# Rotary attention with a squared-ReLU MLP: scale and bias carried inside g, two-step rotations, a new order

## The chip, the cores and the metric

The kernel runs on one core of a Trainium2 chip. TensorE (PE) does the matrix products, and its weight loads are counted apart (PEld). VectorE (DVE), ScalarE (ACT) and GpSimd (POOL) do the elementwise work. SyncE (SP) issues every DMA. The metric is the device time of one execution in microseconds.

## The reference, cut to what matters

```python
# q, k, v: (4, 8, 576, 64); x: 2304 tokens of 512; w_in: 512 x 2048; w_out: 2048 x 512; s, b: one number each
q_rot, k_rot = rotate(q), rotate(k)      # [x1*cos - x2*sin, x1*sin + x2*cos] on halves of 32
attn = softmax(q_rot @ k_rot.T / 8)      # rows of 576
x = (attn @ v) as 2304 x 512
h = x @ w_in
r = max(h, 0)
g = s * (r * r) + b
out = g @ w_out
```

## The kernel before

The 32 (batch, head) pairs are handled two heads at a time, as 16 pairs `pr`. For each pair q, k and v are loaded, q and k are rotated, transposed and multiplied into tiles of 128x576 scores (`s_tile`, `s_pair`). `s_max` (DVE) takes the negated maximum of each row, `s_exp` (ACT) the exponentials and their sums, `p_r` the reciprocals, and `p_a` and `p_b` write each probability as two fp16 halves. DMA transposes turn these round (`p_t`, `p_tt`), and `pv_sum` (PE) multiplies with v, which is split in two halves as well. Pairs 0 to 3 go partly through fp32 products instead.

The weights arrive as 32 loads of 512 KB in 64-bit words and are rebuilt as fp32 (`w_low`, `w_rebias`, `w_join`). `w_gram` and `w_tot` bound their size. After that, `w_hi` and `w_lo` split each fp32 weight in place into two scaled fp16 halves.

The MLP works in nine units `u` of 256 tokens. Unit 0 runs in fp32 while the weights are still fp32: `mlp_in0`, `mlp_r0` (ReLU, then square, on ACT) and `mlp_out0`, in 8 chunks of 128x512. Units 1 to 8 use the halves, and each product is three matmuls. In each of 8 chunks per unit, `mlp_in` writes a 128x512 PSUM bank, `mlp_r` (ACT) makes hr = r squared, `g_hi` (ACT or DVE) rounds it to fp16, `g_lo` (DVE or POOL) subtracts to get the remainder, and `mlp_out` multiplies both by w_out. `out_sum` multiplies the result by a scale and adds the bias row. `x_norm`, `x_add`, `x_sum` and `x_scale` choose the power of two for each unit.

The bias b times the sums of w_out's columns is one row of 512 numbers, made once. `bias_cols` sums the columns of all 32 halves of w_out with matmuls (L510), `bias_part` copies the result out, `bias_mm` adds up the partitions (L517) and `bias_out` puts the row, `bcs`, into SBUF. `add_bias` and `out_sum` use it.

A rotation takes three instructions on one engine: z = x * sin with halves swapped (L589), x = x * cos (L591), x = x + z (L593). The buffer z has two slots.

Every instruction's place is written out by hand in the string ORDER. PICKS says which engine does a piece that has a choice, and SLOTS says which buffer slot a tile takes. Each engine runs its instructions strictly in that order, and a semaphore makes it wait for another engine or a DMA. The scores have two PSUM tiles, the products of the first layer two banks, hr two buffers and g three. The lines L411, L413, L416 and L419 are helpers through which most DVE, POOL and ACT instructions go, so groups are told apart there by their tiles.

Of the kernel before, what the change touches and what calls it, by code (L numbers as in the profile page):

```python
# [21 lines left out]
P_SCALE = 2.0 ** 14  # L22
# [11 lines left out]
BUFS = {"s": 2, "bank": 2, "po": 1, "nat": 1, "ot": 1, "xc": 4, "xt": 1, "hr": 2, "k": 2, "q": 2, "v": 4, "z": 2, "p": 4, "pab": 6, "pt": 2, "x": 4,  # L34
# [40 lines left out]
    "Y2joYCX5j7YMYQkMYRYkYDj1kNYNX7Izj9Y3YgjqYOjyYcYSj0YlYnYdkVYmYokOkEYyYPj8X6kFYzYpj-YEY0YqkUYrkPYvj_YskWYwkHkXaMYtY4ZQYhZR"
    "aNZSY5Y6Y9aPY7kGYikhkIY-Y8kQkikSkjY_aQkkkJkYklkRaRjAkZkTYxkmaOknkokbkpkqkrZTksYuZgkaaSYjktkcn0kdaTaUkukeZUkvZVk4ZWkwZXZb"
    "kxZYk5kykzZjk6n1lWZkk7ZZlXn2k8k9lClYZhlZkflDaVn3k0lEn4k2lFk1lGk-ZllHlAn5Zin6Zck3n7k_n8n9n-lBn_lIZClMZDZFlNZGoAZHZAlOZmZn"
    "lPZoZrZuZalQl0ZvlRZsl1ZpZElJl2ZIZJlLZKZBl3lKZNl4lhZwlalglbZxoMliZyljZOlSZLZzlTZMlrZ0Z-ZdlVldZPlUlclkkgZ1lellZ2lfZ3Z5oLl5"
    "lnoNlqoOoPlmlsoQloZ_ltZeZ6lpZfZ4oglulvZtofZ7lxohoCoiZqoVlzoBl7oDlwoEaBaXlyl9oFl6oGl_oWaCaYl8Z8l-ojmAoIZ9aZaDopoXaWoYoKaA"
# [70 lines left out]
def plan():  # L150
# [32 lines left out]
    def prep(pr):  # L183
# [14 lines left out]
        for nm in "kq":  # L198
            add((DVE, POOL), "rotate", pr, nm, steps=3, r=[("tab",)], w=[(nm, pr), ("z", pr, nm)])
# [893 lines left out]
```

## Time and profile before

| what | value |
|---|---|
| median of 3 runs | 604.07 us (603.09 to 606.6) |
| profiled execution | 603.72 us, of which the span from first to last instruction is 601.9 us |
| PE busy | 575.6 us (96%) |
| DVE busy | 467.4 us (78%) |
| ACT busy | 400.6 us (67%) |
| POOL busy | 143.8 us (24%) |
| granted TensorE clock | 1.00, that is 2.4 GHz |

A busy share is an average over stages. The stretches in the rows below tell the stages apart: the loads and the first pairs, attention together with the MLP, and the MLP alone at the end. Mean durations include the time in which an instruction was held up by another engine. Neighbouring instructions of one engine overlap by a few hundredths of a microsecond, so a sum of durations is a little more than the busy time.

### The profile page before, as it was taken

The page shows a single profiled execution, that of the slowest core. Times are in us where ns is not written, and L with a number is a line of the kernel's source. Part 1 is how long each engine was busy: PE and PEld are TensorE (multiplying, and loading weights), DVE is VectorE, ACT ScalarE, POOL GpSimd, SP SyncE. Part 2 cuts the span into 40 slices and gives each one's busy share as a digit, 9 for nine tenths or more (in the row PEclk, how much of TensorE's full clock was granted, in tenths as well). Part 3 has the DMA queues.
Part 4 walks back from the last instruction along what each step waited for, and adds up shares of the span by engine and source line. Part 5 has one row for each costly group of instructions (what it writes and reads, how often), then busy time and mean ns, then how long its engine had stood idle before and what let it go on. Part 6 is the DMA issues. An engine that isn't in the chain of part 4 may idle for free.

```text
span 601.9 us, 12378 instructions
## 1 busy us (share of the span) xinstructions
PE 575.6 (96%) x4655; PEld 391.7 (65%) x4655; DVE 467.4 (78%) x975; ACT 400.6 (67%) x838; POOL 143.8 (24%) x138
## 2 busy tenths in 40 slices
PE   2799999899999999999999999999999999999997
PEld 1476767566576657666766586666756676666774
DVE  5898999999999999999989999796777752223101
ACT  3798878689899886786868686757656453324321
POOL 0153521334332312331402253100310022120000
PEclk9999999999999999999999999999999999999999
DMA  8999999975975589799778587657654016310100
GB/s 305 307 336 283 221 237 188 214 163 130 214 167 123 126 154 202 158 192 194 152 162 198 125 153 151 156 129 146 120 99 114 2 40 133 95 40 1 36 1 35
DMA packets 210011, 90.32 MB, mean 150 GB/s; under 512 B 192288, under 2 KB 196768, under 8 KB 209952
## 3 DMA queue, kind: packets, MB, share of 16 engines
q1 hardware_dynamic: 209952, 89.54, 64.3%
q8 instruction: 36, 0.59, 0.4%
q14 instruction: 23, 0.19, 0.1%
HBM read 31.97 MB, written 4.72 MB: 61 GB/s over the span
## 4 chain that ended last, share of the span: by engine, by line
PE 83%; DVE 7%; DMA 4%; ACT 3%; issue 2%; POOL 1%; SPq 0%; DVEq 0%; ACTq 0%
PE px L886 28%; PE po L962 25%; PE px L759 8%; PE s L672 8%; PE po L929 4%; PE px L912 4%; DMA x<-in_moe_w_in_dram 2%; DMA x<-in_moe_w_out_dram 2%; PE s L962 2%; DVE wio L416 2%; PE s L654 2%; ACT p L419 1%; PE s L673 1%; DVE pab L416 1%; ACT x L419 1%
## 5 line engine op out<-in xcount | busy, mean ns | idle before, releaser
L886 PE MATMUL px<-xa,wio 128*128 128x256 f16 x1536 | 180.2, 273 | 0.0
L962 PE MATMUL po<-wio,g 128*128 128x512 f16 x720 | 171.9, 379 | 0.5 <-DVE o L416 0.5
L886 PEld LDWEIGHTS <-wio 128*128 128x128 f16 x1536 | 148.0, 98 | 29.6 <-issue 1.6
L419 ACT ACTIVATE p<-s,nm 128x576 f32<-128x576 f32 x144 | 105.5, 734 | 60.1 <-DVE s L681 30.9
L416 DVE SCALAR_TENSOR_TENSOR pab<-p,sum,pab 128x576 f16<-128x576 f32 x136 | 118.7, 887 | 8.1 <-ACT pab L419 4.7
L962 PEld LDWEIGHTS <-g 128*128 128x128 f16 x816 | 75.6, 98 | 73.1 <-issue 3.8
L681 DVE TENSOR_SCALAR_CACHE_REDUCE s<-s,sc 128x576 f32<-128x576 f32 x108 | 87.2, 819 | 17.0 <-PE s L673 15.5
L904 POOL TENSOR_TENSOR g<-hr,g 128x512 f16<-128x512 f32 x36 | 44.5, 1239 | 175.2 <-DVE g L783 85.4
L419 ACT ACTIVATE hr<-px,xc 128x512 f32<-128x512 f32 x64 | 43.5, 681 | 59.3 <-PE px L886 42.1
L413 POOL TENSOR_SCALAR pab<-p,sum 128x576 f16<-128x576 f32 x44 | 38.9, 887 | 165.6 <-DVE sum L708 114.9
L419 ACT ACTIVATE pab<-p,sum 128x576 f16<-128x576 f32 x67 | 50.5, 767 | 18.2 <-DVE sum L708 16.4
L759 PE MATMUL px<-pt,v 128*64 128x320 f16 (+2 forms) x640 | 49.0, 281 | 0.6 <-DVE wmx L480 0.6
L904 DVE TENSOR_TENSOR g<-hr,g 128x512 f16<-128x512 f32 x28 | 19.2, 688 | 36.1 <-ACT g L419 35.8
L419 ACT ACTIVATE hr<-hr 128x512 f32<-128x512 f32 x68 | 42.7, 629 | 1.7
L672 PE MATMUL s<-qkT 128*128 128x512 f16 (+1 forms) x120 | 41.3, 382 | 1.8 <-ACT p L419 1.8
L672 PE MATMUL s<-kS,qkT 128*128 128x512 f16 (+1 forms) x120 | 41.3, 380 | 0.0
L759 PEld LDWEIGHTS <-v 128*64 128x64 f16 x640 | 32.8, 110 | 11.2 <-issue 8.4
L672 PEld LDWEIGHTS <-qkT 128*128 128x128 f16 (+1 forms) x240 | 22.6, 100 | 23.8 <-issue 4.8
L419 ACT ACTIVATE g<-hr 128x512 f16<-128x512 f32 x39 | 24.2, 625 | 13.6 <-PE po L962 10.9
L912 PE MATMUL px<-x,wio 128*128 128x128 f32 x256 | 31.8, 278 | 0.0
L912 PEld LDWEIGHTS px<-x,wio 128*128 128x128 f32 x256 | 30.0, 192 | 2.7 <-issue 1.9
L783 DVE CAST g<-hr 128x512 f16<-128x512 f32 x25 | 10.5, 419 | 23.9 <-PE po L962 15.0
(151 smaller groups left out, 826.3 us busy)
## 6 DMA issues: line engine op xcount, KB each, us to landing
x<-in_moe_w_in_dram SPq DMA_DIRECT2D x16, 512.0 KB, 5.5
x<-in_moe_w_out_dram SPq DMA_DIRECT2D x16, 512.0 KB, 4.7
st_v<-in_v_dram SPq DMA_DIRECT2D x16, 320.0 KB, 3.8
st_q<-in_q_dram SPq DMA_DIRECT2D x16, 288.0 KB, 4.1
st_k<-in_k_dram SPq DMA_DIRECT2D x16, 288.0 KB, 3.9
out_dram<-o SPq DMA_DIRECT2D x7, 512.0 KB, 3.3
kS<-qkT SPq DMA_DIRECT2D x24, 144.0 KB, 2.6
pt<-pab SPq DMA_TRANSPOSE x152, 3.0
```

Of the source, the lines that this page charges most:

```text
L413: eng.tensor_scalar(out=out, in0=in0, scalar1=s1, scalar2=s2, op0=op0, op1=op1)
L416: nc.vector.scalar_tensor_tensor(out=out, in0=in0, scalar=scalar, in1=in1, op0=op0, op1=op1)
L419: nc.scalar.activation(out=out, in_=in_, func=func, **kw)
L654: nc.tensor.matmul(ps[h][:, to], d["qF"][hh, t * P:(t + 1) * P], d["kF"][hh, keys], start=True, stop=True)
L672: nc.tensor.matmul(ps[rows, MAIN:2 * MAIN], lhs, kk[:, h:8:2], start=(n == 0), stop=(n == 1))
L681: nc.vector.tensor_scalar(out=T["s"], in0=T["s"], scalar1=st[pr]["es"], scalar2=None, op0=ALU.mult, op1=ALU.min, accum_out=T["nm"])
L759: nc.tensor.matmul(o[64 * h:64 * h + 64, c], v_rows(pr, h, k, z), p_rows(pr, 2 * (i // 4) + h)[:, k, c], start=((z, k) == todo[0]), stop=( ...
L886: nc.tensor.matmul(ph, w16[0][:, f, wz, cc], X["xa"][:, xz, c], start=(c == 0 and n == 0), stop=(c == NC - 1 and n == 2))
L904: (nc.vector if eng == DVE else nc.gpsimd).tensor_tensor(out=g[:, 1], in0=r, in1=g[:, 0], op=ALU.subtract)
L912: nc.tensor.matmul(ph, wi[:, f + 1, c * P:(c + 1) * P], xs[0]["x"][:, c, j * P:(j + 1) * P], start=(c == 0), stop=(c == NC - 1))
L929: nc.tensor.matmul(X["po"][:, j * DM:(j + 1) * DM], gs["h", j, f - f % 4][:, f % 4 * P:(f % 4 + 1) * P], wo[:, f + 1], start=(n == 1), sto ...
L962: nc.tensor.matmul(po, g[:, gz, jj], w16[1][:, f, wz, to], start=(n == 1 and i == 0), stop=(n == NF and i == 2))
```

## The change

The power of two and the sign in s are folded into the weights' inverse scale, and b, suitably scaled, is added to every element of g before the second product. That makes the sums over w_out's columns superfluous: `bias_cols`, `bias_part`, `bias_mm`, `bias_out` and `add_bias` go, and so does the dependence of `out_sum` on `bcs`. `g_hi` becomes an addition of a per-partition number with a rounding, and `g_lo` becomes (hr + b) - g_hi in one DVE instruction. Unit 0 gets an extra pass `mlp_b0` over each of its 8 chunks. `sb_scale`, 14 instructions on one or two columns in 9 steps, prepares the scales, and `x_scale` grows from 7 steps to 8. `out_sum` is now a plain scaling and may go to ACT.

A rotation now multiplies x, read twice, by a table of cosines and sines side by side into z (128x1152), and one addition of the two halves of z writes x. The table grows from 432 KB to 576 KB, and z becomes one slot of twice the size. The ORDER, PICKS and SLOTS strings are all new.

```diff
-BUFS = {... "z": 2, ...}
+BUFS = {... "z": 1, ...}
...
-            add((DVE, POOL), "rotate", pr, nm, steps=3, r=[("tab",)], w=[(nm, pr), ("z", pr, nm)])
+            add((DVE, POOL), "rotate", pr, nm, steps=2, r=[("tab",)], w=[(nm, pr), ("z", pr, nm)])
...
-    def bias():
-        add(PE, "bias_cols", r=[("w16", 1, f) for f in range(NF)], w=[("bank", "cols")])
-        add(ACT, "bias_part", r=[("bank", "cols")], w=[("bcs",)])
-        add(PE, "bias_mm", r=[("bcs",)], w=[("bank", "bias")])
-        add(ACT, "bias_out", r=[("bank", "bias"), ("wsc", 1)], w=[("bcs",)])
...
+                add((ACT, DVE), "mlp_b0", j, f, r=[("sc0",)], w=[hr])
...
-        add(DVE, "x_scale", u, steps=7, r=[("bank", "xn", u), ("wsc", 0), ("wsc", 1)], w=[("xc", u)])
+        add(DVE, "x_scale", u, steps=8, r=[("bank", "xn", u), ("wsc", 0), ("wsc", 1)], w=[("xc", u)])
...
-            add((ACT, DVE), "g_hi", u, f, r=[("hr", c)], p=[("g", c)])
-            add((DVE, POOL), "g_lo", u, f, r=[("hr", c)], w=[("g", c)])
+            add((ACT, DVE), "g_hi", u, f, r=[("hr", c), ("xc", u)], p=[("g", c)])
+            add(DVE, "g_lo", u, f, r=[("hr", c), ("xc", u)], w=[("g", c)])
...
-            add(DVE, "out_sum", u, j, r=[("pj", u, j), ("bcs",), ("xc", u)], ...)
+            add((ACT, DVE), "out_sum", u, j, r=[("pj", u, j), ("xc", u)], ...)
...
+    add(DVE, "sb_scale", steps=9, r=[("sb",)], w=[("sc0",)])
...
-    tab = const.tile([P, 9, 96], F32, name="tab")
+    tab = const.tile([P, 9, 2, D], F32, name="tab")
...
-        z = new(rp, "z", [P, 9, 2, 32], F32)
-        eng.tensor_tensor(out=z[:, :, ::-1], in0=x, in1=sin, op=ALU.mult)
-        yield
-        eng.tensor_tensor(out=x, in0=x, in1=cos, op=ALU.mult)
-        yield
-        eng.tensor_tensor(out=x, in0=x, in1=z, op=ALU.add)
+        z = new(rp, "z", [P, 9, 2, D], F32)[:, 0:n]
+        eng.tensor_tensor(out=z, in0=x[:, :, None].to_broadcast([P, n, 2, D]), in1=tab[:, g], op=ALU.mult)
+        yield
+        turned = z[:, :, 1].rearrange("p t (h e) -> p t h e", h=2)[:, :, ::-1]
+        eng.tensor_tensor(out=x.rearrange("p t (h e) -> p t h e", h=2), in0=z[:, :, 0].rearrange("p t (h e) -> p t h e", h=2), in1=turned, op=ALU.add)
...
+    def plus(eng, out, x, add):
+        if eng == ACT:
+            act(out, x, AF.Identity, bias=add)
+        else:
+            ts_(out, x, add, ALU.add)
...
-        (nc.vector if eng == DVE else nc.gpsimd).tensor_tensor(out=g[:, 1], in0=r, in1=g[:, 0], op=ALU.subtract)
+        nc.vector.scalar_tensor_tensor(
+            out=g[:, 1], in0=r, scalar=xs[u]["c"][:, 2:3], in1=g[:, 0], op0=ALU.add, op1=ALU.subtract)
...
-        stt(X["o", j], out_tile(u, j), X["c"][:, 1:2], bcs[:, to], ALU.mult, ALU.add)
+        cast(eng, X["o", j], out_tile(u, j), X["c"][:, 1:2])
```

What the new strings say can be counted, with the plan's numbering. The table gives instructions per engine, old to new, for the whole kernel and for two parts of the order: from its beginning to the first `mlp_in` of unit 1, and from there to the 108th `s_max`.

| piece, engine | whole kernel | to the first `mlp_in` | from there to the 108th `s_max` |
|---|---|---|---|
| `g_lo`, POOL | 36 to 0 | 0 | 21 to 0 |
| `g_lo`, DVE | 28 to 64 | 0 | 6 to 26 |
| `g_hi`, DVE | 25 to 21 | 0 | 12 to 3 |
| `rotate`, DVE | 81 to 50 | 39 to 26 | 36 to 19 |
| `rotate`, POOL | 15 to 14 | 9 to 7 | 6 to 7 |
| `out_sum`, `out_sum0`, `add_bias`, DVE | 19 to 8 | 0 | 8 to 3 |
| `out_sum`, ACT | 0 to 10 | 0 | 0 to 4 |
| `mlp_b0`, ACT | 0 to 8 | 0 to 8 | 0 |
| `w_low`, DVE | 5 to 10 | 5 to 10 | 0 |
| `p_a`, DVE | 25 to 23 | 4 to 0 | 11 to 9 |
| `p_a`, POOL | 44 to 52 | 11 to 13 | 17 to 25 |

The first DMAs of the old order are q of pair 0, the table with the identity matrix, and k of pair 0. In the new order the table and the identity come first, then q and k. On DVE the old order begins with the rotation steps q0, q1, k0, q2, k1, a `w_join`, k2; the new one with q0, q1, k0, k1, `w_join`. In the new order six of POOL's seven rotations are followed by one on DVE that needs the same z. The closest of these is pair 11: between the place of POOL's rotation of k and that of DVE's rotation of q, DVE has four `s_max`, one `p_r` and one `g_lo` to do.

## Rows read from the trace of the kernel before

**Rows 1.** Busy time of each engine by stretch: start:end, length, PE, PEld, DVE, ACT, POOL.

```profile
0.00:25.00 25.00, 9.94 (x49) 6.26 (x50) 17.73 (x30) 12.79 (x23) 2.66 (x6) 1.00 0.86 300
25.00:125.00 100.00, 95.46 (x859) 69.03 (x859) 95.99 (x191) 79.40 (x182) 35.47 (x34) 1.00 0.94 246
...
150.00:375.00 225.00, 222.99 (x1854) 148.23 (x1854) 214.88 (x462) 177.65 (x378) 65.56 (x59) 1.00 0.79 166
375.00:475.00 100.00, 100.00 (x788) 65.59 (x784) 77.76 (x169) 64.35 (x132) 13.84 (x15) 1.00 0.55 115
...
sum 602.00, PE 575.56 PEld 391.69 DVE 467.37 ACT 400.56 POOL 143.81; mean PE 82.22 PEld 55.96 DVE 66.77 ACT 57.22 POOL 20.54
```

**Rows 2.** Chain that ended last, first 130 us: start, length, what.

```profile
27.94 7.28 DMA x<-in_moe_w_in_dram
```

**Rows 3.** Instructions in order of time, first 15 us: start, length, engine, line.

```profile
4.77 0.76 DVE L589 TENSOR_TENSOR z<-st_q,tab 128x576 f32<-128x576 f32 x1 [3.60 <-DMA tab<-in_rope_dram]
...
7.88 0.76 DVE L589 TENSOR_TENSOR z<-st_k,tab 128x576 f32<-128x576 f32 x1 [1.56 <-DMA st_k<-in_k_dram]
...
11.01 0.75 DVE L593 TENSOR_TENSOR st_k<-st_k,z 128x576 f32<-128x576 f32 x1
...
11.82 1.12 PE L766 MATMUL s<-ident,st_k 128*128 128x128 f32 x4 [0.93 <-DVE st_k L593]
...
14.09 2.40 PE L654 MATMUL s<-qkT 64*128 64x512 f32 x8 [0.75 <-ACT qkT L419]
```

**Rows 4.** Instructions of PE in order of time, 213 to 220 us.

```profile
213.42 1.91 PE L510 MATMUL px<-wio,ones 128*32 128x512 f16 x32
215.66 0.38 PE L672 MATMUL s<-qkT 128*128 128x512 f16 x1 [0.33 <-ACT p L419]
...
217.19 0.27 PE L851 MATMUL px<-g,ones16b 128*128 128x256 bf16 x1 [0.24 <-ACT bcs L419]
...
218.44 1.02 PE L517 MATMUL px<-bcs,ones 128*128 128x512 f32 x2
219.30 2.10 PE L962 MATMUL po<-wio,g 128*128 128x512 f16 x9
```

**Rows 5.** Groups by line and form: count, busy us, mean ns, idle before.

```profile
L416 DVE SCALAR_TENSOR_TENSOR pab<-p,sum,pab 128x576 f16<-128x576 f32 x136 | 118.7, 887 | 8.1 <-ACT pab L419 4.7 <-POOL pab L413 2.9
...
L681 DVE TENSOR_SCALAR_CACHE_REDUCE s<-s,sc 128x576 f32<-128x576 f32 x108 | 87.2, 819 | 17.0 <-PE s L673 15.5 <-ACT hr L419 1.2
...
L904 POOL TENSOR_TENSOR g<-hr,g 128x512 f16<-128x512 f32 x36 | 44.5, 1239 | 175.2 <-DVE g L783 85.4 <-ACT g L419 72.0 <-DVE sum L708 7.2
...
L416 DVE SCALAR_TENSOR_TENSOR wio<-wio,wsc 128x512 f16<-128x512 f32 x32 | 26.8, 838 | 0.8 <-ACT wio L419 0.8
...
L419 ACT ACTIVATE g<-hr 128x512 f16<-128x512 f32 x39 | 24.2, 625 | 13.6 <-PE po L962 10.9 <-PE px L851 1.3 <-PE s L962 1.0
...
L904 DVE TENSOR_TENSOR g<-hr,g 128x512 f16<-128x512 f32 x28 | 19.2, 688 | 36.1 <-ACT g L419 35.8
...
L589 DVE TENSOR_TENSOR z<-st_k,tab 128x576 f32<-128x576 f32 x15 | 12.8, 850 | 1.6 <-DMA st_k<-in_k_dram 1.6
...
L416 DVE SCALAR_TENSOR_TENSOR o<-po,xc,bcs 128x512 f32<-128x512 f32 x15 | 11.1, 747 | 7.3 <-PE po L962 6.5 <-DMA out_dram<-o 0.8
...
L783 DVE CAST g<-hr 128x512 f16<-128x512 f32 x25 | 10.5, 419 | 23.9 <-PE po L962 15.0 <-ACT hr L419 8.9
...
L416 DVE SCALAR_TENSOR_TENSOR xa<-x,xs,xa 128x1024 f16<-128x1024 f32 x7 | 8.9, 1276 | 0.9 <-ACT xa L419 0.8
...
L589 POOL TENSOR_TENSOR z<-st_q,tab 128x576 f32<-128x576 f32 x4 | 6.6, 1645 | 3.0 <-DMA st_q<-in_q_dram 2.9
```

**Rows 6.** Instructions of DVE in order of time, 422 to 428 us.

```profile
421.83 0.81 DVE L416 SCALAR_TENSOR_TENSOR pab<-p,sum,pab 128x576 f16<-128x576 f32 x1
...
423.60 3.95 DVE L416 SCALAR_TENSOR_TENSOR pab<-p,sum,pab 128x576 f16<-128x576 f32 x3
```

**Rows 7.** Instructions of POOL in order of time, same stretch.

```profile
423.22 2.98 POOL L904 TENSOR_TENSOR g<-hr,g 128x512 f16<-128x512 f32 x2
```

More of the change, by code (lines that the diff above doesn't have):

```diff
@@ L280, in halve @@
             add(PE, "w_tot", which, r=[("top", which)], w=[("bank", "tot", which)])
-            add(DVE, "w_scale", which, steps=4, r=[("bank", "tot", which)] + ([("sb",)] if which else []), w=[("wsc", which)])
+            add(DVE, "w_scale", which, steps=4, r=[("bank", "tot", which), ("sc0",)], w=[("wsc", which)])
         old = [("w32", which, f - 1)] if f else [("w32", 0, NF - 1)] if which else []
@@ L284, in halve @@
         add(DVE, "w_lo", which, f, r=[("w32", which, f), ("wsc", which)], w=[("w16", which, f)])
-    def bias():
-        add(PE, "bias_cols", r=[("w16", 1, f) for f in range(NF)], w=[("bank", "cols")])
-        add(ACT, "bias_part", r=[("bank", "cols")], w=[("bcs",)])
-        add(PE, "bias_mm", r=[("bcs",)], w=[("bank", "bias")])
-        add(ACT, "bias_out", r=[("bank", "bias"), ("wsc", 1)], w=[("bcs",)])
-        for j in range(2):
-            add(DVE, "add_bias", j, r=[("bcs",), ("sb",)], w=[("o", 0, j)], p=[("ot", 0)])
-        add(DMA, "store", 0, (0, 1), r=[("o", 0, 0), ("o", 0, 1), ("ot", 0)])
     def unit0():
@@ L344, in plan @@
             halve(which, f)
-    bias()
     for u in range(1, NU):
@@ L448, in load_w, with sb_scale @@
         wst[which, f] = t
+    def sb_scale():
+        d, root, zero, sigma, b1, mag = (sc[:, i:i + 1] for i in range(6))
+        stt(mag, sb[:, 0:1], -1.0, sb[:, 0:1], ALU.mult, ALU.max)
+        yield
+        yield from pow2(d, mag, root)
+        ts_(zero, mag, 0.0, ALU.is_equal)
+        yield
+        ts_(root, root, 2.0 ** 13, ALU.mult)
+        stt(root, zero, 0.0, root, ALU.is_equal, ALU.mult)
+        ts_(d, d, 2.0 ** -13, ALU.mult)
+        yield
+        stt(sigma, sb[:, 0:1], d, d, ALU.mult, ALU.mult)
+        yield
+        nc.vector.tensor_tensor(out=sigma, in0=sigma, in1=zero, op=ALU.add)
+        yield
+        nc.vector.reciprocal(b1, sigma)
+        nc.vector.tensor_tensor(out=b1, in0=b1, in1=sb[:, 1:2], op=ALU.mult)
+        nc.vector.memset(xw[:, 0:1], 1.0 + 2.0 ** -6)
+        nc.vector.memset(xb[:, 0:1], 0.0)
+        stt(mag, b1, -1.0, b1, ALU.mult, ALU.max)
+        ts_(sc[:, 6:7], root, 1.0 / P_SCALE, ALU.mult)
+        ts_(xb[:, 1:2], mag, 4096.0 * (1.0 + 2.0 ** -6), ALU.mult, 2.0 ** -100, ALU.add)
     def w_low(which, f, eng):
@@ L504, in w_lo @@
         stt(d[:, 1], w32[which][:, f + 1], wsc[:, which:which + 1], d[:, 0], ALU.mult, ALU.subtract)
-    def bias_cols():
-        o = wst["b"] = bank()
-        for n in range(2 * NF):
-            g = slice(32 * (n % 4), 32 * (n % 4) + 32)
-            nc.tensor.matmul(o[g], ones16, w16[1][:, n // 2, n % 2], start=(n < 4), stop=(n >= 2 * NF - 4))
-    def bias_part():
-        act(bcs, wst["b"], AF.Copy, scale=1.0 / 32.0)
-    def bias_mm():
-        wst["b"] = bank()
-        nc.tensor.matmul(wst["b"], ones32, bcs, start=True, stop=True)
-    def bias_out():
-        act(bcs, wst["b"], AF.Copy, scale=sb[:, 3:4])
     st = {pr: {} for pr in range(NPAIR)}
```

177 lines of the change are left out of this document (88 added, 89 removed).

## The prediction

> **What bounds the kernel now.** I read the busy times by stretch first [rows 1]. The reader is to see three regimes. In the first 25 us PE works 9.9 us: it waits for the first loads and rotations. From 25 to 125 us PE is busy 95.5 of 100 us while DVE is busy 96.0 and the DMA engines 0.94, so three resources are full together. From 150 to 375 us PE is busy 223.0 of 225 and DVE 214.9; from 375 to 475 us PE is busy 100.0 of 100 while DVE falls to 78. The granted clock is 1.00 in every stretch, that is 2.4 GHz. PE is idle for about 26 us in all (601.9 less 575.6 [rows 1]), and more than half of that lies in the first 25 us. So time is gained by giving PE less to do, or by filling its holes in the first 125 us. Work added to DVE costs nothing after 375 us, and before that it has 10 us of room in 225.
>
> The chain that ended last says the same of the early part: it leads through loads of the weights, one of which takes 7.28 us from issue to landing [rows 2]. A load starts when a buffer comes free, so in this part DMA, ACT and DVE take turns in setting the pace.
>
> **The change part by part.** The sum is made against the profiled execution, 603.72 us, 0.35 under the median of the runs.
>
> *The bias row.* PE spends 1.91 us on `bias_cols` and 0.86 us from the start of `bias_mm` to that of the next matmul, and `x_sum` waits 0.24 us for the bank that ACT's `bcs` copy still reads [rows 4]. That is 3.0 us of PE at most. The matmul after `bias_cols` was held 0.33 us by ACT all the same [rows 4], so I take 2.7. The lower end is 1.1 (0.86 + 0.24), if the wait for ACT had lasted as long without `bias_cols`. From 375 us on PE has no idle time, so what it saves before that reaches the end: -2.7 us (-3.0 to -1.1).
>
> *The start.* The table is a third larger and now goes first, with q and k behind it, so the first rotation, which waited 3.60 us for the table, starts later: the 144 KB more are, at the 300 GB/s of this stretch [rows 1], 0.5 us. Against that, k's rotation took from 7.88 to 11.76 us because a step of q and a `w_join` stood between its steps [rows 3]. Now its two steps stand together and take about 1.38 + 0.75 us after a landing at about 8.4 us, so k's transposes start near 10.5 instead of 11.82 and the first score tile near 12.8 instead of 14.09 [rows 3]. The ends are -1.3 us and +0.5 us (the later table, and the loads behind it setting the pace [rows 2]); I take -0.5.
>
> *The early stretch, up to unit 1.* DVE loses a third of its rotation steps there (39 to 26). A set of three takes 3 x 0.75 = 2.25 us undisturbed [rows 3]. The new z step has 1152 elements; the nearest rows are 0.75 us for 576 and 1.28 us for 1024 elements [rows 3, 5]. The line through them gives 1.42; the ends are 1.28 and 2 x 0.75. I take 1.4, so a set takes 2.15 and 13 sets save 1.3 us. Five more `w_low` against four fewer `p_a` on DVE, all one-input instructions like the cast of 0.42 us [rows 5], give +0.4, and the 14 small instructions of `sb_scale` at most 0.42 each, more likely half of it: +3 us. That nearly cancels, +2 on 96. On ACT the eight `mlp_b0` cost 8 x 0.63 = 5.0 us [rows 5], beside 79.4 of 100 us used [rows 1]. Behind each `mlp_b0` on ACT's queue stand exponentials, and PE's `mlp_out0` waits for it; the cover is the score tiles and `w_gram` that PE has between. I take 0, with ends at +5.0 (no cover) and -4.5 (the whole PE idle time of this stretch [rows 1]).
>
> *The tight stretch, 160 to 375 us.* Here DVE counts. Up to the 108th `s_max` it has 20 more `g_lo`, and all are three-operand: 26 at 0.69 to 0.84 us, the latter being the row of the same form with its hold-ups; I take 0.76. Against six at 0.69 [rows 5] that is +15.6 us (+13.8 to +17.7). Rotations: 36 steps at 0.75 make 27.0 us; nine and a half sets of 2.15 make 20.4: -6.6. Eight bias additions at 0.75 become three one-input copies at 0.42 to 0.75 [rows 5]: -4.2. Nine fewer `g_hi` at 0.42 [rows 5]: -3.8. Two fewer `p_a`: -0.8. The sum is about 0, with ends at +3 and -2. So the subtractions come to DVE without a net load, and ACT takes the rest: nine `g_hi` at 0.63 and four `out_sum` at about the same are +8 us on 178 of 225 [rows 1, 5], where it has room.
>
> POOL loses 36 subtractions of 1.24 us [rows 5], 45 us. It gains eight `p_a`, about 6 us at DVE's 0.8 for such an instruction, and its seven rotations, with z up to twice the 1.65 us that 576 elements take [rows 5], make 7 x 4.95 = 35 us against 15 steps of 1.65 or 25 us. That matters to DVE: a `p_b` takes 0.81 us alone, but three in a row took 3.95 us while two POOL subtractions of 2.98 us together ran [rows 6, 7]. Over all 136 the mean is 0.89, that is 0.08 x 136 = 10 us of hold-up for 144 us of POOL work [rows 1, 5]. POOL will work some 29 us less (45 - 6 - 10), so about 2 us come back on DVE. The Trainium skill has a rule for this ("SBUF — State Buffer", section "Who interferes with whom"): a DVE instruction with two SBUF inputs contends with a GpSimd instruction that reads SBUF, and whichever issued second fully blocks. By the rows 2 us come back; by that rule every overlapping pair would cost a whole instruction, and the 36 subtractions gone could return up to 36 x 0.81 = 29 us. It also speaks against the change, since the new `g_lo` and the twice as long z step are themselves two-input. The row agrees that single instructions are blocked (3.95 us against 3 x 0.81).
>
> For PE I take -0.5 in this stretch; the most is its 2.0 us of idle time [rows 1], and the other end is +3.
>
> *The end* is left out: the last product, scaling and store follow one another as before, on PE at full speed.
>
> The sum: 603.72 - 2.7 - 0.5 + 0 - 0.5 = 600.0 us, or 600.4 beside the median of 604.07.
>
> **The rivals.** *The single z buffer ties POOL to DVE (slower).* A rotation on POOL now holds the only z for 1.65 + 3.3 us and its waits [rows 5], and the next rotation on DVE, a strict queue with the maxima behind it, must wait. At pair 11 DVE has four `s_max` at 0.82, a `g_lo` and a `p_r` to do meanwhile, about 4.2 us [rows 5]. If POOL takes longer than that, each microsecond over it stands on DVE where it is 96% full, and PE runs out of scores. Such a handover occurs six times; at two of them a full 5 us would be 10 us: 610 us. It decides from two stalls of about 3.5 us on. For it speaks that POOL's own instructions are held up too; against it, that most handovers seem to have far more work between them.
>
> *The saved PE time is eaten (same).* PE lacks 2.7 us of work, but the new order has its holes elsewhere, for instance behind the eight `mlp_b0`: half of their 5.0 us without cover leaves 600.4 + 2.5 = 602.9, all of it 605.4.
>
> *More than PE's own saving (faster).* If DVE gets back several microseconds from POOL and the first tile's 1.3 us carries through, the holes between 25 and 125 us (4.5 us) and in the tight stretch (2.0 us) close as well [rows 1]: 603.72 - 3.0 - 1.3 - 4.5 - 2.0 makes 593; half of the gain beyond the forecast, 597.
>
> **How the numbers follow.** About 0.5%, or 3 us, is what a measurement of this kernel can tell from no change; so faster is under 601.05 and slower over 607.1. The forecast (598 to 603) has 0.44, of which 0.28 is faster; saved time eaten (602 to 606) 0.20; the single z, or another new stall of that size (607 to 612), 0.20; the larger gain (593 to 598) 0.16. That gives 0.45 faster, 0.35 same, 0.20 slower. The range leaves out the lower part of the larger gain and the upper of the stalls: 594.5 to 608.5. The likeliest case's own range is 598 to 603.
>
> **What would show it.** Right: no PE work at lines of bias sums; the first score tile before 13.5 us; a z step on DVE near 1.4 us; DVE's `g_lo` at 0.7 to 0.8 us; DVE busy between 475 and 600 us clearly more than now, and PE full from 150 us on. Wrong: waits of DVE's z step on POOL of microseconds; PE idle before `mlp_out0` for ACT; PE idle of more than 5 us between 150 and 475 us. The prediction fails on the fast side if the holes in the first 125 us shrink by more than 2 us, since I give the new order no credit there.

## The result and the profile after

The changed kernel takes 607.66 us (median of 14 runs, 605.23 to 610.75) against 603.84 us (14 runs beside them). The ratio is 1.0074 [1.0051, 1.0098]: slower by about 4.5 us (the two medians lie 3.8 apart). The forecast was 600.4 us, faster. The profiled execution has a span of 608.0 us and 609.82 us in all, 2.2 over the median.

The busy times by stretch, which answer to [rows 1], come first (columns as there; behind POOL stand the granted clock, the DMA share and GB/s):

```profile
0.00:25.00 25.00, 11.99 (x65) 7.77 (x66) 18.32 (x28) 12.15 (x22) 1.60 (x5) 1.00 0.92 331
25.00:125.00 100.00, 94.46 (x829) 69.90 (x831) 92.04 (x195) 85.44 (x192) 34.68 (x30) 0.98 0.93 235
150.00:375.00 225.00, 218.43 (x1776) 144.26 (x1776) 209.81 (x439) 176.15 (x373) 56.42 (x50) 1.00 0.85 165
375.00:475.00 100.00, 99.71 (x800) 65.80 (x799) 81.78 (x183) 60.55 (x129) 14.19 (x16) 1.00 0.57 113
...
475.00:550.00 75.00, 73.31 (x579) 50.20 (x578) 33.93 (x70) 31.91 (x61) 0.74 (x1) 1.00 0.38 67
```

PE does 2.0 us more than before in the first 25 us. Between 25 and 125 us it does 1.0 us less, and the clock is 0.98. Most of the new idle time lies between 150 and 375 us: 6.6 us without work instead of 2.0. DVE is *less* busy there (209.8 against 214.9), so it isn't the sum of DVE's work that holds PE. Another 1.7 us, where there was none, lies between 475 and 550. Other cuts of the same view narrow it down; first the kernel before, then the changed one:

```profile
0.00:60.00 60.00, 43.37 (x363) 30.76 (x363) 50.13 (x97) 42.85 (x94) 16.09 (x21) 1.00 0.90 308
...
150.00:300.00 150.00, 147.99 (x1218) 98.09 (x1217) 144.28 (x314) 122.69 (x256) 43.80 (x41) 1.00 0.81 170
```

```profile
0.00:60.00 60.00, 43.36 (x341) 31.56 (x343) 47.85 (x91) 40.71 (x87) 16.21 (x17) 0.97 0.85 295
...
150.00:300.00 150.00, 143.52 (x1152) 94.37 (x1152) 141.53 (x291) 120.92 (x254) 43.85 (x37) 1.00 0.84 164
```

Up to 60 us PE's busy time is the same to 0.01 us, though the changed kernel began earlier: the gain of the start is gone by then. Between 150 and 300 us it lacks 4.5 us.

Equal busy time isn't equal work here. The rows' 1.00 does not hold for the first 30 us, in either kernel: the trace has no record of the clock before 29.66 us in the old kernel and 31.00 us in the changed one, and a stretch without a record is printed as 1.00. What PE's clock was shows in equal groups of matmuls, here in the changed kernel:

```profile
26.37 2.07 PE L789 MATMUL po<-dg,p 128*128 128x128 f32 x8
...
31.20 1.16 PE L789 MATMUL po<-dg,p 128*128 128x128 f32 x8
```

So PE works at 1.2 GHz up to about 30 us (in the old kernel such a group takes 1.16 us from 29.89 us on). Up to the first record it was busy for 17.99 us in the changed kernel and for 14.49 in the old one. Busy time at 1.2 GHz counts half as work, and the changed kernel has 3.4 us of it once more behind 44 us, so by 60 us it is behind by an estimated 3 us of work (half of 17.99 + 3.4 - 14.49); the rows show 341 matmuls instead of 363.

The largest hole between 150 and 300 us ends at 264.51 us. The instructions of POOL, DVE and PE around it, in order of time:

```profile
255.88 3.20 POOL L585 TENSOR_TENSOR z<-st_k,tab 128x1152 f32<-128x1152 f32 x1
259.16 1.50 POOL L588 TENSOR_TENSOR st_k<-z 128x576 f32<-128x576 f32 x1
```

```profile
256.51 2.89 DVE L403 TENSOR_SCALAR pab<-p,sum 128x576 f16<-128x576 f32 x1
259.32 3.42 DVE L408 SCALAR_TENSOR_TENSOR pab<-p,sum,pab 128x576 f16<-128x576 f32 x3
262.66 0.81 DVE L676 TENSOR_SCALAR_CACHE_REDUCE s<-s,sc 128x576 f32<-128x576 f32 x1
```

```profile
264.51 0.38 PE L667 MATMUL s<-qkT 128*128 128x512 f16 x1 [3.15 <-ACT p L411]
```

While POOL computes the new z (pair 11, k), one `p_a` of DVE lasts 2.89 us and ends within 0.3 us of POOL's instruction. The three `p_b` behind it take 3.42 us, and only then comes the `s_max` for which ACT's exponential and PE wait. Two more holes have the same ahead of them: z on POOL at 89.38 us (3.24 us) beside a `w_join` on DVE of 3.11 us, ahead of a hole of 1.92 us at 95.6; and at 157.09 us (2.62) beside a `p_b` of 2.95 us, ahead of a hole of 1.36 us at 163.5. The first ends like the largest one; behind the second PE waits not for scores but for `xa`, the halves of x that DVE makes for `mlp_in`:

```profile
97.49 1.08 PE L656 MATMUL s<-qkT 64*64 64x512 f32 x4 [1.92 <-ACT p L411]
```

```profile
164.83 1.36 PE L884 MATMUL px<-xa,wio 128*128 128x256 f16 x11 [1.36 <-DVE xa L408]
```

The three holes make 6.4 us.

The early hole, at 41.28 us, has another origin. DVE first:

```profile
27.90 0.75 DVE L588 TENSOR_TENSOR st_k<-z 128x576 f32<-128x576 f32 x1
31.32 1.42 DVE L674 TENSOR_REDUCE nm<-s 128x1 f32<-128x576 f32 x2 [2.67 <-PE s L649]
...
33.78 1.12 DVE L408 SCALAR_TENSOR_TENSOR wio<-x,wio 128x512 uint32<-128x512 uint32 x1
```

then the DMA queue, and PE:

```profile
28.43 0.38 SPq L528 DMA_DIRECT2D st_k<-in_k_dram  x1
34.93 0.33 SPq L439 DMA_DIRECT2D x<-in_moe_w_in_dram  x1
35.31 0.42 SPq L528 DMA_DIRECT2D st_q<-in_q_dram  x1
35.83 0.37 SPq L439 DMA_DIRECT2D x<-in_moe_w_in_dram  x1
```

```profile
43.57 0.63 PE L492 MATMUL px<-wio 128*128 128x128 bf16 x8 [2.29 <-DVE wio L408]
```

DVE waits 2.67 us for scores, which PE computes at 1.2 GHz (eight matmuls in 2.27 us from 29.00; eight of the same line take 1.30 at 91.39), with a `w_join` queued behind; the join (33.78) gives a buffer back only at 34.9, so no load is issued for 6 us, and the tile that PE needs at 41.3 comes late. Behind this hole the clock falls (windows of 2 us, same columns):

```profile
42.00:44.00 2.00, 0.43 (x8) 0.44 (x8) 1.18 (x3) 1.94 (x5) 1.79 (x2) 1.00 1.02 409
44.00:46.00 2.00, 2.00 (x12) 1.39 (x9) 2.00 (x5) 1.55 (x7) 1.25 (x2) 0.66 0.82 145
46.00:48.00 2.00, 2.00 (x20) 1.88 (x19) 1.50 (x3) 2.00 (x5) 2.00 (x1) 0.50 0.95 272
48.00:50.00 2.00, 2.00 (x17) 1.47 (x18) 1.92 (x6) 2.00 (x5) 0.92 (x2) 0.98 0.90 271
```

PE is busy all the time, but between 44 and 48 us mostly at 1.2 GHz: 2.00 x (0.34 + 0.50 + 0.02) = 1.7 us of work lost. The kernel before showed no fall behind the first 30 us. Over the executions, the core's mean granted clock is 0.9951 (14) against 0.9989 for the kernel before (26 beside the first experiments): 0.0038 x 603 = 2.3 us.

### The profile page after: what moved, and what is told of

It is laid out like the page before. It is cut to its first block, busy times and chain, and to the rows that moved or that the text cites. A ratio compares the mean times of both kernels' runs of the same rounds, so it can differ in the third digit from the quotient of the medians.

```text
span 608.0 us, 12290 instructions
## 1 busy us (share of the span) xinstructions
PE 576.9 (95%) x4621; PEld 393.7 (65%) x4621; DVE 474.3 (78%) x986; ACT 409.1 (67%) x854; POOL 112.8 (19%) x107
## 4 chain that ended last, share of the span: by engine, by line
PE 68%; DVE 15%; DMA 9%; SPq 3%; issue 3%; ACT 2%; DVEq 0%; ACTq 0%
PE px L884 24%; PE po L967 20%; PE px L754 7%; PE s L667 6%; DMA pt<-pab 4%; DVE pab L408 3%; DVE wio L408 2%; PE px L917 2%; DMA x<-in_moe_w_in_dram 2%; PE po L938 2%; PE s L967 2%; DVE z L585 2%; SPq L733 1%; DVE nm L674 1%; DVE s L676 1%
## 5 line engine op out<-in xcount | busy, mean ns | idle before, releaser
L408 DVE SCALAR_TENSOR_TENSOR pab<-p,sum,pab 128x576 f16<-128x576 f32 x136 | 113.5, 848 | 11.4 <-ACT pab L411 6.8
L405 POOL TENSOR_SCALAR pab<-p,sum 128x576 f16<-128x576 f32 x52 | 45.7, 883 | 252.3 <-DVE sum L703 210.8
L908 DVE SCALAR_TENSOR_TENSOR g<-hr,xc,g 128x512 f16<-128x512 f32 x64 | 49.8, 782 | 38.7 <-ACT g L411 38.1
L411 ACT ACTIVATE pab<-p,sum 128x576 f16<-128x576 f32 x61 | 46.2, 767 | 14.3 <-DVE sum L703 8.6
L411 ACT ACTIVATE g<-hr,xc 128x512 f16<-128x512 f32 x43 | 30.7, 717 | 12.6 <-PE po L967 7.2
L667 PEld LDWEIGHTS <-qkT 128*128 128x128 f16 (+1 forms) x240 | 22.3, 100 | 24.9 <-issue 6.2
L668 PEld LDWEIGHTS <-qkT 128*128 128x128 f16 (+1 forms) x240 | 22.0, 100 | 10.2 <-issue 4.8
L674 DVE TENSOR_REDUCE nm<-s 128x1 f32<-128x576 f32 x36 | 26.3, 747 | 3.0 <-PE s L649 2.7
```

Source lines behind the costliest of these rows:

```text
L405: eng.tensor_scalar(out=out, in0=in0, scalar1=s1, scalar2=s2, op0=op0, op1=op1)
L408: nc.vector.scalar_tensor_tensor(out=out, in0=in0, scalar=scalar, in1=in1, op0=op0, op1=op1)
L411: nc.scalar.activation(out=out, in_=in_, func=func, **kw)
L667: nc.tensor.matmul(ps[rows, MAIN:2 * MAIN], lhs, kk[:, h:8:2], start=(n == 0), stop=(n == 1))
L668: nc.tensor.matmul(ps[rows, MAIN - TAIL:MAIN], lhs, kk[:, 8, 64 * h:64 * h + 64], start=(n == 0), stop=(n == 1))
L674: nc.vector.tensor_reduce(out=T["nm"], in_=T["s"], axis=AX.X, op=ALU.max, negate=True)
```

## The experiments

Theories: **L**, POOL's long z holds one DVE instruction for its whole length, at places where what PE needs next (scores, or `xa`) stands behind it. **G**, its rival: DVE now carries all 64 `g_lo` and is too full. **Q**, the early hole comes from the late `w_join`; **D**, its rival: the early stretch is set by when data arrive, and a closed hole opens elsewhere. **C**: the clock falls because of PE's hole. **B**: PE's saved time isn't worth anything. Each ratio is to the kernel before on the same chip.

**z on POOL in two halves.** Two instructions of 576 elements instead of one of 1152.

```diff
+        if e == DVE:
+            eng.tensor_tensor(out=z, in0=x[:, :, None].to_broadcast([P, n, 2, D]), in1=tab[:, g], op=ALU.mult)
+        else:
+            for i in range(2):
+                eng.tensor_tensor(out=z[:, :, i], in0=x, in1=tab[:, g, i], op=ALU.mult)
```

> The changed kernel, except that on POOL alone the wide z step is issued as two instructions of 576 elements (about 1.65 us each) in the same place. Theory L: a single POOL instruction of 2.6 to 3.2 us holds the port that DVE needs, so DVE stands for up to 3 us at once and PE runs dry (holes of 1.9, 1.4 and 3.2 us near 96, 163 and 261 us in the changed kernel). Halved, the longest hold on DVE falls below 2 us and these holes together from 6.4 to under 3 us: 603 to 605.5 us, 0.999 to 1.003 of before. Theory G: the loss comes from DVE carrying all 64 subtractions for the remainder of g; then nothing changes: 1.006 to 1.009.

608.24 us, ratio 1.0082 [1.0056, 1.0108]: no gain, L as stated there missed. POOL, then DVE:

```profile
255.18 3.49 POOL L589 TENSOR_TENSOR z<-st_k,tab 128x576 f32<-128x576 f32 x2
```

```profile
255.74 1.66 DVE L403 TENSOR_SCALAR pab<-p,sum 128x576 f16<-128x576 f32 x1
257.33 4.57 DVE L408 SCALAR_TENSOR_TENSOR pab<-p,sum,pab 128x576 f16<-128x576 f32 x3
```

The halves follow one another without a gap, and each holds one DVE instruction: 1.66 instead of 2.89 us, but the `p_b` behind take 4.57 instead of 3.42. The four together take 6.23 us instead of 6.31, and the hole ahead of the scores stays (3.16 us). What is held here is the sum of POOL's time, however it is cut.

**All rotations on DVE.**

```diff
+    for x in work:
+        if x["fn"] == "rotate":
+            pick[x["fn"], x["a"]] = DVE
```

> The changed kernel, except that POOL's seven rotations go to DVE in the same places of the order; nothing else moves. Theory L: no DVE instruction is held longer than 2 us any more, and PE's holes near 96, 163 and 261 us close; DVE gets 7 x 2.1 = 15 us more work, so part of it comes back as small waits: 602 to 606 us, 0.997 to 1.004 of before. Theory G: DVE is too full already, and 15 us more make it worse than the changed kernel: 1.010 to 1.020.

604.84 us, 1.0040 [1.0016, 1.0064]. DVE has more to do and the kernel is faster. The same place, DVE and then PE, and below it the stretch from 150 us:

```profile
255.56 0.51 DVE L403 TENSOR_SCALAR pab<-p,sum 128x576 f16<-128x576 f32 x1
255.99 2.27 DVE L408 SCALAR_TENSOR_TENSOR pab<-p,sum,pab 128x576 f16<-128x576 f32 x3
258.18 1.35 DVE L585 TENSOR_TENSOR z<-st_k,tab 128x1152 f32<-128x1152 f32 x1
259.44 0.82 DVE L676 TENSOR_SCALAR_CACHE_REDUCE s<-s,sc 128x576 f32<-128x576 f32 x1
```

```profile
261.30 0.38 PE L667 MATMUL s<-qkT 128*128 128x512 f16 x1 [0.89 <-ACT p L411]
```

```profile
150.00:300.00 150.00, 146.54 (x1175) 95.91 (x1174) 143.96 (x308) 123.75 (x259) 27.29 (x29) 1.00 0.85 167
```

With z itself on DVE (1.35 us) the `s_max` begins at 259.44 instead of 262.66, PE's hole falls from 3.15 to 0.89 us (that at 95 us to 0.50; that at 163 us is gone, with one of 0.75 behind it at 166), and PE's busy time from 150 to 300 us rises by 3.0 of the 4.5 us lost. The two ratios' intervals overlap, but the same change was run three times more below. L holds; G falls.

**36 of the `g_lo` back on POOL** (the same tiles as before; their bias is left out).

```diff
+        if (u, f) in ON_POOL:
+            nc.gpsimd.tensor_tensor(out=g[:, 1], in0=r, in1=g[:, 0], op=ALU.subtract)
+        else:
...
```

> The changed kernel, except that the 36 subtractions for g's remainder that POOL did in the kernel before are done there again (as r minus g, so the bias is left out of these remainders). Theory L: the holes near 96, 163 and 261 us stay, since the wide z steps stay, and POOL's subtractions of 1.2 us add holds of their own on DVE: 607 to 612 us, 1.005 to 1.013 of before. Theory G: DVE is relieved of about 27 us, and the time falls by 3 us or more against the changed kernel: 0.995 to 1.002.

609.80 us, 1.0111 [1.0078, 1.0144]: G falls again, relieving DVE does not help. The stretch from 150 us, then the `p_b`, first in the changed kernel and then in this run:

```profile
150.00:375.00 225.00, 218.63 (x1763) 143.55 (x1762) 206.68 (x418) 174.51 (x371) 80.24 (x71) 0.99 0.84 163
```

```profile
L408 DVE SCALAR_TENSOR_TENSOR pab<-p,sum,pab 128x576 f16<-128x576 f32 x136 | 113.5, 848 | 11.4 <-ACT pab L411 6.8 <-POOL pab L405 3.9
```

```profile
L411 DVE SCALAR_TENSOR_TENSOR pab<-p,sum,pab 128x576 f16<-128x576 f32 x136 | 122.0, 912 | 13.5 <-ACT pab L414 8.9 <-POOL pab L408 4.1
```

The mean `p_b` grows from 848 to 912 ns, 8.7 us of hold-up over 136, and yet PE is busy 218.6 us from 150 to 375 as without them (218.4). So many short hold-ups spread over the stretch left PE as it was; but DVE also has the 36 `g_lo` less to do, about 28 us, so the run doesn't show that the hold-ups alone would cost nothing. That the ratio is 0.37% above the changed kernel's is within the two intervals.

**The kernel before without its bias sums**, in its own order: `bias_cols` and `bias_mm` are empty, `bcs` is zero, so b is missing from the output.

> The kernel before in its old order, with the sums over the second weight matrix left out (both matmul groups and both copies; the bias row is zero, so b is missing from the output). Prediction's first term: PE's 2.7 us come off one to one: 601 us, 0.9935 to 0.9975 of before. Rival: the time saved on PE is eaten by a wait that ends at the same moment anyway: 0.998 to 1.002.

602.37 us, 0.9982 [0.9954, 1.0010]: at most a gain of 2.8 us, by the middle 1.1, so nearer to the rival than to the full term. PE, and the clock behind it:

```profile
213.51 0.58 PE L668 MATMUL s<-qkT 128*128 128x512 f16 x1 [2.19 <-ACT p L419]
```

```profile
210.00:215.00 5.00, 2.81 (x15) 1.29 (x14) 4.96 (x14) 3.79 (x10) 0.07 (x1) 0.84 0.94 211
215.00:220.00 5.00, 5.00 (x24) 2.07 (x21) 4.34 (x15) 3.40 (x8) 2.15 (x3) 0.82 0.66 152
```

Before, `bias_cols` ran ahead of this score tile, which then waited 0.33 us for ACT [rows 4]. Without it the wait is 2.19 us, and the clock falls behind it.

**Joins forward.** Five items of the order are moved up; each line says what, and ahead of what.

```diff
+MOVES = (
+    (('w_join', 0, 4), ('s_max', 1, 2)),
+    (('w_rebias', 1, 1), ('s_exp', 1, 2)),
+    (('w_low', 1, 1), ('s_exp', 1, 2)),
+    (('w_join', 1, 1), ('w_max', 0, 0)),
+    (('load_w', 0, 5), ('s_exp', 1, 2)),
+)
...
```

> The changed kernel with five items moved forward in its order, all between 27 and 36 us: the `w_join` of weight tile (0, 4) ahead of `s_max` (1, 2), `w_rebias` and `w_low` of (1, 1) ahead of `s_exp` (1, 2) on ACT, `w_join` (1, 1) behind the second `s_max`, and `load_w` (0, 5) up with the first. The computation is the whole one. Theory Q (a free buffer is handed back late: DVE stands 2.67 us at `s_max` with the join queued behind it, so no load starts between 28.8 and 34.9 us, PE misses the tile for 2.29 us at 41.3 us, and the granted clock then falls): the load starts near 28.8 us, PE's hole at 41.3 us shrinks below 1 us, the granted clock between 40 and 50 us is at least 0.97 again (0.83 in the changed kernel), and the time is 2 to 4 us below the changed kernel: about 604 to 605.5. Rival D (DMA or the arrival of the later tiles sets this stretch anyway, and the clock's fall has nothing to do with this hole): the hole moves or stays, the time stays at 607 to 608.

609.23 us, 1.0108 [1.0085, 1.0131]. Q fails here (windows in which PE is full left out):

```profile
30.00:35.00 5.00, 2.58 (x34) 2.23 (x32) 4.44 (x10) 3.10 (x9) 4.15 (x4) 1.00 0.84 275
...
40.00:45.00 5.00, 2.83 (x27) 1.84 (x26) 4.97 (x12) 4.59 (x13) 2.18 (x2) 1.00 0.88 270
...
50.00:55.00 5.00, 3.63 (x48) 3.06 (x46) 4.17 (x12) 5.00 (x12) 1.53 (x2) 1.00 0.75 211
```

The clock stays at 1.00 there, but PE now has three holes (2.4, 2.2 and 1.4 us): the join waited until 30.2 us for ACT's `w_low` and held the maxima, and the later tile was late all the same.

**Joins forward and all rotations on DVE.**

> The same five items forward, and all rotations on DVE (none on POOL). The computation is the whole one. If the early hole (theory Q) and DVE held by POOL's wide rotation steps (theory L, 3 us in the run with rotations on DVE) are two separate losses, the gains add: 607.7 - 3 - 3 = 600 to 602.5, faster than before by 1 to 3 us, with no PE hole over 1 us behind 35 us. Rival: they overlap, since PE catches up in the same later waits, and the time stays near that of the rotations on DVE alone, 604 to 605.

606.42 us, 1.0056 [1.0034, 1.0079]: 0.52% below the same order with POOL's rotations, so L's gain comes again. Moving the joins gave nothing to add to it, and the kernel is not faster than before.

**No `mlp_b0`** (the eight passes empty; the bias is missing from the hidden values of unit 0).

> The changed kernel without the eight `mlp_b0` passes; the bias is missing from the hidden values of unit 0. The rival of the prediction that the saved PE time is eaten by these passes (5.0 us of ACT, no cover): 2.5 to 5 us below the changed kernel, 603 to 605. My theory (they lie under other work, the losses are the early hole and POOL's holds): within 1 us of the changed kernel, 606.7 to 608, PE's holes at 41, 95, 163 and 261 us still there.

607.15 us, 1.0069 [1.0047, 1.0092]: 0.05% from the changed kernel, with holes of 1.91, 1.59, 1.35 and 3.15 us at the four places. These passes are covered; that rival of the prediction falls.

**ACT's part forward as well.** `w_rebias` and `w_low` (0, 4) stand ahead of `p_ev` (0, 0), the first join ahead of `s_max`, the second behind the first `w_max`.

> The changed kernel with another set of items forward. The run with `w_join` (0, 4) ahead of `s_max` only moved the hole, because the join waited for ACT's `w_low` of the same tile until 30.2 us and held the maxima behind it. Here `w_rebias` and `w_low` (0, 4) stand ahead of the copy of `p_ev` (0, 0) on ACT, in 1.56 us in which ACT waited for PE, so the join is done near 29.4 us, before the scores are there; `load_w` (0, 5) follows it, `w_rebias` and `w_low` (1, 1) stand ahead of `s_exp` (1, 2), and `w_join` (1, 1) behind the first `w_max`. The computation is the whole one. Theory Q (the late hand-back of one buffer makes the early hole, and the hole the fall of the clock): no PE hole above 1 us between 25 and 60 us, clock 1.00 there, and 2 to 3.5 us below the changed kernel, 604 to 605.7. Rival D (this stretch is set by the sum of its DMA, ACT and DVE work, so a hole closed opens another): holes of 2 us or more in all remain between 25 and 60 us, time 606.5 to 609.

608.07 us, 1.0082 [1.0060, 1.0105]. The loads follow one another sooner (DMA share 0.73 from 30 to 35 us instead of 0.39), and still PE has holes of 2.17 us at 39.8 and 1.44 at 49.6. Two repairs of the order did not shorten the stretch, which speaks for D; that the arrival of the tiles is the cause was not tried by itself.

**The same, and six of the seven rotations on DVE.**

> The same items forward, and six of POOL's seven rotations on DVE; that of q of pair 3 stays on POOL, where DVE stood idle beside it. The computation is the whole one. By theories Q and L together: 600.5 to 602.5, at or a little below the kernel before, PE's holes behind 25 us under 8 us in all. By rival D the early holes remain and the time is 604 to 606, as with all rotations on DVE.

604.62 us, 1.0026 [1.0011, 1.0040], 0.56% below the run above: L a third time, and the time that rival D named. PE's early holes are 1.23 us at 39.9 and 2.30 at 43.1.

**PE's early hole filled, rotations on DVE.** Ahead of `w_gram` (0, 3) PE computes the sums of `w_gram` (0, 2) five more times, each started afresh.

```diff
+        again = (which, f) == (0, 3)
+        for i in range(5 if again else 0):
+            y = top16(w32[0][:, 3])
+            for c in range(NC):
+                cc = y[:, c * P:(c + 1) * P]
+                nc.tensor.matmul(o, cc, cc, start=(c == 0), stop=(c == NC - 1 and i < 4))
...
```

> The changed kernel with all rotations on DVE, and in PE's early hole (1.76 us at 41.0 us in that run, ahead of `w_gram` (0, 3)) 20 matmuls of `w_gram` (0, 2) again, whose sums are started afresh and so stay the same. Theory C (the fall of the granted clock to 1.2 GHz between 43 and 47 us is brought on by PE's hole; the hole itself costs nothing more that can be had): the clock stays at 1.00 between 40 and 50 us, about 1.2 us of idle time become busy time, and the profiled span falls by up to 1.5 us, with a time 0.7 to 1.5 below the run with rotations on DVE: 603.3 to 604.1. Rival: the clock falls all the same, or the repeats delay the chain; 604.8 to 606.

604.66 us, 1.0028 [1.0011, 1.0045], short of the 603.3 to 604.1 expected. In its profile the next hole (2.25 us at 44.7) is followed by a fall to 0.80 instead. Over the 12 executions the mean clock is 0.9993, against 0.9982 with the rotations on DVE alone and 0.9988 of the kernel before: 0.0011 x 603 = 0.7 us, and the ratio fell by as much, well within the intervals. With the clock of the kernel before, it is still slower by 0.28%.

**PE's early hole filled in the changed kernel**, seven times instead of five.

> The changed kernel with 28 such matmuls in its early hole (2.29 us at 41.3 us); its holes at 95, 163 and 261 us are left. Theory C: the clock stays at 1.00 between 40 and 50 us, the mean clock of its executions rises from 0.995 by about 0.002, and the time falls by 1 to 1.7 us to 606 to 606.7. Rival: no fall, 607.5 or more.

607.49 us, 1.0070 [1.0046, 1.0094], not the 606 to 606.7 expected. The profiled execution:

```profile
40.00:45.00 5.00, 4.13 (x50) 3.30 (x50) 3.72 (x7) 3.76 (x9) 2.23 (x2) 1.00 0.97 329
45.00:50.00 5.00, 4.62 (x50) 4.00 (x48) 5.00 (x13) 4.52 (x12) 3.92 (x2) 1.00 0.82 263
```

Here the clock stays at 1.00 where the changed kernel had 0.96 and 0.69. One profile can't show that the filling did it: with 36 `g_lo` on POOL the early hole stood unfilled (2.42 us at 41.2), and the clock stayed at 1.00 behind it too. Over the eight executions the mean is 0.9960 against 0.9951, and the time falls by 0.04%, within the error. For C speaks that every fall in the profiles stands behind a hole of PE (last section); that filling this one removes a fall is not shown, and it is worth under 1 us.

**PE's time put back.** 13 matmuls, whose product nobody reads, ahead of `pv_sum` (7, 3).

```diff
+        if (pr, i) == (7, 3):
+            for n in range(13):
+                nc.tensor.matmul(o, w16[1][:, 0, 0, 0:P], w16[1][:, 1, 0], start=True, stop=True)
```

> The changed kernel with 13 matmuls of 128x512 float16 put back on PE at 211 us, ahead of `pv_sum` (7, 3), two microseconds before the place where `bias_cols` and `bias_mm` ran in the kernel before: 13 x 0.216 = 2.8 us of PE time, whose product nobody reads. Theory of the prediction (PE sets this stretch, so what it saves there reaches the end): 2.8 us over the changed kernel, a ratio to before near 1.012. Theory B (the saved PE time is eaten by later waits for ACT and DVE, which have as much to do as before: without the bias sums the old order gained 1.1 of 2.7 us): at most 1.7 us over it, a ratio of 1.0075 to 1.010.

609.78 us, 1.0131 [1.0108, 1.0154]; the matmuls ran from 209.25 us for 2.97 us:

```profile
209.25 2.97 PE L750 MATMUL px<-wio 128*128 128x512 f16 x13
```

0.57% or 3.4 us more (by the two intervals, 1.4 to 5.4). B, which allowed 1.010 at most, falls: in the new order PE's time in this stretch reaches the end, by the middle in full.

## Why the prediction was wrong

The range held 607.66; the sign and the likeliest case were wrong. The step that failed is in the tight stretch, POOL's contention, "so about 2 us come back on DVE". It took the hold-up as a mean over all of POOL's busy time, by which less work on POOL is a gain, and so put the tight stretch at -0.5; PE's idle time there grew by 4.6 us. What counted was *one* instruction, its length and what stands behind it on DVE: three z of 2.6 to 3.2 us, two ahead of scores and one ahead of `xa`, made holes of 6.4 us in the profile. With the rotations off POOL the ratio fell in four pairs of the same order: 1.0074 to 1.0040, 1.0108 to 1.0056, 1.0082 to 1.0026, 1.0070 to 1.0028; the mean is 0.46%, or 2.8 us. More than half of it is the clock: the mean granted clock rose in these pairs by 0.0031, 0.0022, 0.0025 and 0.0033, about 1.7 us. In six of the eight profiles with POOL's z the clock fell to 1.2 GHz behind the hole at 261 us; in the changed kernel's own it did not. The prediction had the row that shows it ([rows 6, 7]: three `p_b` in 3.95 us beside POOL's 2.98) and averaged it away. The Trainium skill ("SBUF — State Buffer", section "Who interferes with whom") says that of a DVE and a GpSimd instruction that contend the one that issues second fully blocks. The trace agrees: the `p_a` began 0.6 us behind POOL's z, ended 0.3 us behind it and took 2.89 us instead of 0.51. From this rule the prediction worked out up to 29 us for the 36 `g_lo`, at 0.81 us for each, the length of the DVE instruction; what the rows show as the price of a blocked pair is the rest of the POOL instruction. With the 36 back on POOL the `p_b` were held 8.7 us longer in all.

*The bias row* (-2.7, lower end 1.1). In the old order the middle is 1.1 (0.9982 x 603.84 less 603.84), the lower end: the wait for ACT that `bias_cols` had filled came back. In the new order, 2.8 us of PE put back cost 3.4 (1.4 to 5.4). So the saving is there, and the term stands.

*The start* (-0.5). Right in itself: the first score tile starts at 13.35 us instead of 14.09. But nothing of it is left at 60 us, where PE's busy time is 43.36 against 43.37 us and more of it was worked at 1.2 GHz. The prediction read 1.00, or 2.4 GHz, for every stretch [rows 1]; in the first 30 us that was wrong, and what PE does earlier there it does at half the speed.

*The early stretch* (0, ends +5.0 and -4.5). The ends were for `mlp_b0` and for PE's idle time, and `mlp_b0` proved to be covered (0.05%). Zero was the second step that failed: PE's idle time between 25 and 125 us grew by 1.0 us, and the lower clock behind the hole at 41 us took 1.7 us of work in the profile. The late join that stops the loads for 6 us stands ahead of that hole, but moving it left holes of the same size, so what causes them stays open.

*DVE's sums* were right: z on DVE 1.35 us (forecast 1.4), `g_lo` 0.78 (0.76), and DVE's busy time from 150 to 375 us did not rise (209.8 against 214.9). The z on POOL took 2.80 us (five) and 3.22 us (two), under the 3.3 forecast.

```profile
L585 DVE TENSOR_TENSOR z<-st_k,tab 128x1152 f32<-128x1152 f32 x14 | 19.1, 1364 | 0.1
...
L585 POOL TENSOR_TENSOR z<-st_q,tab 128x1152 f32<-128x1152 f32 x5 | 14.0, 2795 | 31.3 <-ACT p L411 20.6 <-DVE st_k L588 9.9 <-POOL v L405 0.7
L585 POOL TENSOR_TENSOR z<-st_k,tab 128x1152 f32<-128x1152 f32 x2 | 6.4, 3222 | 0.1
```

*The rivals.* The single z buffer wasn't the wait: ahead of DVE's z of k there is 0.1 us of idle time in all, and that of q waits for DMA. The sign named beforehand, PE idle for more than 5 us between 150 and 475 us, is there (6.6 and 0.3), with the same instruction on POOL as its cause, by another way. The case "or another new stall of that size" stood with a chance of 0.20.

*The two profiles side by side*, 608.0 us of span against 601.9. PE's idle time is 31.0 us instead of 26.3: 2.0 less in the first 25 us, 4.6 more between 150 and 375, 1.7 more between 475 and 550, 0.5 more in the rest. The 1.7 are mostly holes at 533 and 544 us (0.83 and 0.85), where `pv_sum` waits for transposes of p by DMA; with rotations on DVE these waits are smaller (0.34 at 529). PE's busy time is 577.0 us instead of 575.6 although the 2.9 us of bias sums are gone, 4.3 us more for the same matmuls. Of these 1.7 are the fall behind 44 us, and an estimated 1.75 the start, half of the 3.5 us more that PE worked there at 1.2 GHz. About 0.8 us has no place.

*What stays open.* The forecast missed by 7.3 us. 2.8 are POOL's rotations, the clock that rose with their move included; 0.4 is the clock that is still lower with rotations on DVE (0.9982 against 0.9989); 0.5 is the start. For the rest, some 3.5 us, no run shows the cause. The early stretch is a candidate: with rotations on DVE, and PE's time at 1.2 GHz again counted as half, PE is still an estimated 2 us of work behind at 60 us. With all rotations on DVE and the clock of the kernel before, the new order is still 0.28% slower, although PE has 2.8 us less to do. The strings of the order are all new, and no run had the old order with the new instructions. No version that was run is faster than the kernel before.

## What to carry to other kernels

Cost an instruction on POOL by its full length on the one DVE instruction that meets it, and look what stands behind that one in DVE's queue; seven rotations moved off POOL gave 2.8 us here, more than half of it by the granted clock, while thirty-six short ones put back left PE's busy time as it was (with DVE relieved of them). Splitting the long one doesn't help while the parts follow one another; moving it does. A gain at the start counts only if the stretch behind it can use it: compare what PE has done up to the point where the loads stop being the limit, and look at the length of equal matmuls before taking a printed clock of 1.00 for full speed. Take a PE hole for dearer than its length.

## What had not been expected of the hardware

Until about 30 us PE works at 1.2 GHz in both kernels, though the profile prints 1.00 there: eight equal matmuls take 2.07 us at 26.37 and 1.16 at 31.20.

After PE had stood idle the granted clock fell to 0.50 (1.2 GHz) for some time although PE was busy again: behind 2.29 us at 41.3 us in the changed kernel, 2.19 at 211 in the kernel before without bias sums, 1.76 at 41.0 with rotations on DVE, 1.75 at 40.5 and 3.16 at 260.5 with z in halves; each time about 1.5 to 1.7 us of work were lost. Not every hole did it: in the changed kernel's profile the clock was 1.00 behind 1.92 us at 95.6 and 3.15 us at 261.4, and with 36 `g_lo` on POOL behind 2.42 us at 41.2. In the fourteen profiles every fall during the work stands behind a hole of PE, of 1.75 us at the least. The kernel before, whose largest hole behind the first 25 us is 1.58 us at 114, shows no fall.

That POOL's two-input instruction holds a DVE instruction with a single tensor input (the `p_a`, 0.51 us alone, 2.89 beside it) had not been expected either; the forecast had spoken of two-input ones.
